# Second stage of a two-layer attention and S4D kernel: convolutions and the kernels' transform on sixteen 32x32 tiles of TensorE

## The chip, the core and the metric

One of the eight NeuronCores of a Trainium2 chip runs the whole program. Its engines work side by side, each through its own queue in order: TensorE multiplies matrices (PE; its weight loads are PEld), ScalarE (ACT) and VectorE (DVE) work on rows of 128 partitions, GpSimd (POOL) does the same from SBUF alone, and SyncE (SP) issues most of the DMAs. The metric is the device time of one execution in microseconds; what counts is the median of several runs.

## The reference, cut to what matters

A sequence of 2048 positions and 640 channels goes through attention (32 heads of 20), an S4D layer, attention, an S4D layer. Each layer adds its result to x.

```python
def _B_ref(u, log_A_real, A_imag, C_real, C_imag, log_dt, D_skip):
    L = u.shape[1]
    dt = jnp.exp(log_dt)
    A = -jnp.exp(log_A_real) + 1j * A_imag
    C = (C_real + 1j * C_imag) * dt[:, None]
    P = jnp.exp((A * dt[:, None])[:, :, None] * pos[None, None, :])
    K = 2.0 * jnp.einsum("dn,dnl->dl", C, P).real
    L2 = 2 * L
    Kf = jnp.fft.rfft(K, L2)
    Uf = jnp.fft.rfft(u_t, L2)
    y = jnp.fft.irfft(Uf * Kf[None, :, :], L2)[:, :, :L]
    return y + u * D_skip[None, None, :]

x = x + _A_ref(_layernorm(x, axis=-1), A_wqkv, A_wo)
x = x + _B_ref(_layernorm(x, axis=-1), ...)
x = x + _A_ref(_layernorm(x, axis=-1), A_wqkv, A_wo)
x = x + _B_ref(_layernorm(x, axis=-1), ...)
```

The convolution kernel K (640 x 2048) depends on the parameters alone and is the same in both S4D layers. The inputs here make none of its parts vanish, so it is computed in full.

## The kernel before

The program runs in six stretches: the first attention, with `kgen` (K by powers of A, written to the DRAM tensor `kd`) woven into it; the first output projection `out_proj`, with `ktransform` (the Fourier transform of K) woven into it; the first convolution `ssm`; the second attention; its output projection; the second convolution.

**The convolution.** The transform of length 4096 is done in two stages over 16 sub-sequences. Channels come in five blocks of 128 (`b`, NCT = 5), and a block has 32 groups of four channels, taken four groups at a time: eight steps per block (`q`), forty in all (`n`). In `ssm`, a step holds

- `stage1`: twelve matmuls against `e1` (float16, high and low parts) give a pair of sub-sequences of the next block; ACT casts the high part into `x1`, DVE subtracts for the low part;
- `stage2a`: eight transposes of `x1` into PSUM (`pst`, pool T), copied by ACT into `xt`;
- `stage2b`: three matmuls of the 128x128 matrix `f2` with 512 columns of `xt` (`psx`, pool F). `f2` holds a 32x32 matrix four times over, once for each of four channels, and zeros elsewhere. Then the product with the kernel's transform, whose two halves `ka` and `kb` are loaded from `kha` and `khb` (256 KB each): DVE shuffles and multiplies, POOL multiplies and adds, giving `t1`;
- `stage3`: the inverse's first part, four float32 matmuls against `fa` (`psv`, pool M), copied by ACT into `v`;
- `stage4`: the inverse's second part, every other step, sixteen matmul passes on four sub-sequences against `eb` (`psy`, pool M). DVE adds the result to x and, in the first convolution, takes the statistics of the next layer norm; in the second, SP writes the output.

`stage2b` runs one step behind the transposes, `stage3` three, `stage4` eleven.

**The kernels' transform.** `ktransform` does the same first two stages for K, once, in float32 where `ssm` has float16 pairs: transposes by time (`pkt` from `kl`, L1245), the first stage (`pkx`, L1257), transposes (`pkt` from `kx`, L1265), the second stage (`pkf`, L1273), two shuffles and a sign on ACT into `kn`, and 512 KB writes to `kha` and `khb`.

**What sets the order.** Instructions are emitted in the order of the code, and a scheduler then places them on each engine by when it expects them ready, unless they are tied: `tie(made, before)` fixes that one instruction comes after another on its engine. In the attentions everything is tied by a plan. `out_proj`, `ktransform` and `ssm` were not tied: `weave(1000)` emits the whole transform after row 2 of the projection, and the scheduler mixes it with the projection's rows. A generator that is woven gives up control at each `yield`; `weave(1)` advances it by one step.

In the profile a tile name without its number stands for all its buffers, and L78 is the helper `Ordered`, through which most operations of ACT, DVE, POOL and SP go.

## Time and profile before

| what | us |
|---|---|
| three runs | 2668.82, 2673.26, 2675.07 |
| their median | 2673.26 |
| the profiled execution | 2672.17 |
| its span, first to last instruction | 2670.4 |
| first attention (0 to 1091) | 1091.0 |
| first projection, transform of K, layer norm (1091 to 1275.4) | 184.4 |
| first convolution (1275.4 to 1416) | 140.6 |
| second attention and projection (1416 to 2509.7) | 1093.7 |
| last layer norm, second convolution, output (2509.7 to 2670.4) | 160.7 |

Of the span, PE is busy for 2528.2 us (95%), ACT for 2368.0 (89%), DVE for 1511.7 (57%), POOL for 824.4 (31%). The stretches are cut at the first transposes of a convolution (`pst`, L1395), at its last `psy`, and at the ends of the attentions' matmuls. A group's row gives its engine, operation, what it writes and reads, the shape, and after the bar its busy time in us and the mean duration of one in ns. A duration holds the passage through the engine too, and the next instruction may start before it is over; what a piece costs an engine is read from start to start.

### The profile page before, as it was taken

To read this page: it belongs to the slowest core of one execution; us is meant where nothing else is said; L and a number is where in the kernel's file an instruction comes from. 1 tells how busy PE (TensorE), PEld (TensorE's weight loads), DVE (VectorE), ACT (ScalarE), POOL (GpSimd) and SP (SyncE) were. 2 spreads that over 40 slices of the span, in tenths; PEclk is the share of its full clock that TensorE was granted. 3 is DMA by queue.
4 is the path that set the end of the run, shared out by engine and by line. 5 is a ranking of instruction groups with operands and counts; after the bars stand their busy time and mean duration, and the time that the engine had idled before them with its cause. 6 is when DMAs were issued, how large, how long until landed. Compare 5 with 4: busy or idle time off the path is not lost.

```text
span 2670.4 us, 116325 instructions
## 1 busy us (share of the span) xinstructions
PE 2528.2 (95%) x51106; PEld 1424.3 (53%) x51106; DVE 1511.7 (57%) x3451; ACT 2368.0 (89%) x2793; POOL 824.4 (31%) x1256
## 2 busy tenths in 40 slices
PE   7899999999999998999999999999999998999898
PEld 3445444444444443678896444454444443444788
DVE  7687778778855884477776323232233221154864
ACT  7899999999999999676655899999999999998564
POOL 1123334233332334301671122322222222222376
PEclk9999999999999999999999999999999999999999
DMA  6523222222221223554542111121121112222465
GB/s 210 182 52 86 59 78 71 75 61 70 63 54 49 55 64 93 191 231 158 186 151 63 47 53 50 53 58 47 43 63 38 54 32 92 70 67 64 143 189 161
DMA packets 186580, 242.18 MB, mean 91 GB/s; under 512 B 43376, under 2 KB 128976, under 8 KB 184400
## 3 DMA queue, kind: packets, MB, share of 16 engines
q1 hardware_dynamic: 150048, 188.35, 21.7%
q0 software_dynamic: 36016, 46.30, 7.0%
q8 instruction: 403, 6.60, 1.0%
q14 instruction: 113, 0.93, 0.1%
HBM read 158.50 MB, written 76.01 MB: 88 GB/s over the span
## 4 chain that ended last, share of the span: by engine, by line
ACT 58%; PE 21%; issue 11%; DVE 3%; DMA 2%; POOL 1%; SPq 0%; ACTq 0%; POOLq 0%; DVEq 0%
ACT pt L78 56%; PE psv L1420 3%; PE psy L1430 3%; PE pa L893 2%; PE psx L1408 2%; PE S L859 2%; PE psx L1385 1%; PE po L1313 1%; PE pst L1395 1%; PE pkf L1273 1%; PE m L611 1%; PE po L1308 1%; PE pq L764 1%; PE pkx L1257 1%; PE pkt L1265 1%
## 5 line engine op out<-in xcount | busy, mean ns | idle before, releaser
L78 ACT ACTIVATE pt<-S 128x1024 f32<-128x1024 f32 x2048 | 1927.8, 1034 | 34.3 <-PE S L859 22.3
L893 PE MATMUL pa<-pt,V 64*32 64x512 f32 x16384 | 1097.5, 590 | 0.2 <-DVE oc L78 0.2
L859 PE MATMUL S<-qop,kop 61*32 61x512 f16 x16384 | 877.7, 381 | 84.7 <-ACT pt L78 67.6
L859 PEld LDWEIGHTS <-kop 61*32 61x32 f16 x16384 | 366.9, 90 | 737.5 <-issue 617.9
L893 PEld LDWEIGHTS pa<-pt,V 64*32 64x32 f32 x16384 | 313.7, 106 | 70.9 <-issue 10.0
L78 POOL DMA_DIRECT2D dn<-oc x252 | 123.8, 498 | 604.6 <-DVE oc L78 580.1
L78 DVE TENSOR_SCALAR qc<-m 128x512 f32<-128x512 f32 (+1 forms) x68 | 46.8, 688 | 285.2 <-PE m L611 282.7
L78 POOL DMA_DIRECT2D db<-dn x252 | 127.0, 510 | 131.6 <-DMA dn<-dr 128.6
L78 DVE COPY oc<-pa 128x512 f32<-128x512 f32 x64 | 44.2, 690 | 197.9 <-PE pa L893 186.9
L78 POOL DMA_DIRECT2D ot<-oc x256 | 130.1, 516 | 81.3 <-DVE oc L78 49.9
L611 PE MATMUL m<-xh,wh 64*32 64x512 f16 x2560 | 144.7, 379 | 2.4 <-DVE qc L78 2.4
L611 PE MATMUL m<-xh,wl 64*32 64x512 f16 x2560 | 145.8, 378 | 0.0
L611 PE MATMUL m<-xl,wh 64*32 64x512 f16 x2560 | 144.3, 378 | 0.0
L611 PEld LDWEIGHTS <-wh 64*32 64x32 f16 x5120 | 90.7, 94 | 76.3 <-issue 34.6
L78 POOL DMA_DIRECT2D dn<-dr x63 | 35.0, 555 | 302.6 <-DVE dr L78 283.9
L78 ACT COPY xt<-pst 128x1024 f16<-128x1024 f16 x80 | 81.6, 1023 | 47.2 <-PE pst L1395 46.7
L1413 POOL TENSOR_TENSOR t<-t,kb 128x512 f32<-128x512 f32 x80 | 101.9, 1275 | 67.7 <-DVE t L78 66.7
L78 DVE TENSOR_SCALAR V<-m 128x160 f32<-128x160 f32 x64 | 20.7, 324 | 161.6 <-PE m L577 161.6
L78 DVE TENSOR_TENSOR kb<-ktab 128x512 f32<-128x512 f32 x160 | 106.2, 682 | 0.0
L577 PEld LDWEIGHTS <-xh 128*128 128x128 f16 x960 | 79.5, 98 | 45.9 <-issue 29.9
L1414 POOL TENSOR_TENSOR t<-t,t 128x512 f32<-128x512 f32 x78 | 99.2, 1271 | 8.5 <-DVE t L78 2.6
L329 PEld LDWEIGHTS m<-kb,ka 128*32 128x32 f32 x3840 | 61.3, 110 | 73.8 <-issue 55.8
(305 smaller groups left out, 4015.3 us busy)
## 6 DMA issues: line engine op xcount, KB each, us to landing
ka<-kha SPq DMA_DIRECT2D x80, 256.0 KB
kb<-khb SPq DMA_DIRECT2D x80, 256.0 KB
db<-dn POOLq DMA_DIRECT2D x252, 64.0 KB, 3.0
kop<-ks SPq DMA_DIRECT2D x176, 80.0 KB
kpw<-wd POOLq DMA_DIRECT2D x60, 192.0 KB, 4.5
qop<-qs SPq DMA_DIRECT2D x256, 40.0 KB
ot<-oc POOLq DMA_DIRECT2D x256, 40.0 KB, 2.8
kha<-kn SPq DMA_DIRECT2D x20, 512.0 KB
```

The costliest lines, as they stand in the source:

```text
L78: made = f(out, *a, **k)
L329: chain(te.matmul(ps[32 * j:32 * j + 32, c8, :], a[n][:, ch, :], b[n][:, dd, :], start=(n == 0), stop=(n == 2), tile_position=(0, 32 * j)))
L577: chain(te.matmul(ps[:, :n], a_[:, ct, sl], m[:, ct, :], start=(k == 0), stop=(k == 14)))
L611: chain(te.matmul(ps[r][32 * t:32 * t + 32, :], a_[rows, ct, 32 * u:32 * u + 32], m[rows, ct, 512 * v:512 * v + 512], start=(k == 0), stop ...
L764: te.matmul(pq, a_[:, ct, :], m[:, ct, sl], start=(n == 0), stop=(n == 14))
L859: chain(te.matmul(S[32 * t:32 * t + 32, 512 * r:512 * r + 512], kt_[rows, kc + 32 * t:kc + 32 * t + 32], qt[rows, :], start=True, stop=Tru ...
L893: chain(te.matmul(pa[r][32 * j:32 * j + 32, :], V[rows, kt, VP * h:VP * h + 32], pts[j // 2][rows, 512 * (j % 2):512 * (j % 2) + 512], sta ...
L1408: te.matmul(px, f2[:, f, :], xt[:, k, :], start=(n == 0), stop=(n == 2))
L1413: ge.tensor_mul(t2, t2, kb)
L1414: (ge if g0 else ve).tensor_add(t1, t1, t2)
L1420: te.matmul(pv[:, g].rearrange("p r i c -> p (r i c)"), t1[:, g * P:g * P + P], fa, start=True, stop=True)
L1430: te.matmul(py[:, i, :], eb[:, 4 * i4 + i, r, :], v[:, r, 4 * i4 + i].rearrange("p g c -> p (g c)"), start=(r == 0), stop=(r == 1))
```

## The change

It touches `ktransform`, `out_proj`, `ssm`, `prefetch`, the constants and, a little, `kgen`.

1. **Sixteen tiles.** The transposes take their groups with a stride (`of_group`), so that the four channels of a group fall into four blocks of 32 partitions. The second stage (`sets` in `ssm`, `ends` in `ktransform`) then multiplies 32x32 matrices at sixteen positions of the array, four row blocks times four column blocks, with 512 columns each. One set in `ssm` is 48 small matmuls in three passes and stands in place of four steps' twelve matmuls; its result fills four PSUM banks (`F0` to `F3`), for which pool T is gone: `pst` now shares pool X with the first stage.
2. **No shuffles in the transform.** `kha` and `khb` are produced by matmuls with two constant matrices; ACT and DVE only copy.
3. **Equal steps.** In `ssm` every engine's order is fixed by `at`. `stage4` works on two sub-sequences in each step instead of four in every other. The inverse's first part runs six steps behind the transposes (two behind the product), the second part fourteen. `xt` and `t2` have one buffer, `ka` five, and the product is written over `ka`.
4. **The transform step by step.** In `out_proj` each eighth projection matmul advances `ktransform` by one of its seventy steps, and the matmuls and transposes of both are tied into one chain on PE; what is left follows the last row. `kl`, `f2` and the skip weights of the first block are loaded before the first attention ends.
5. In `kgen` the scale of K (`bound`) is computed two blocks later.

```diff
-    kha = dram.tile([P, D // 4, P], F32, name="kha")
+    kha = dram.tile([2 * NCT, P, 4, 4, P], F32, name="kha")
...
+    def matmul(*a, **k):
+        chain(te.matmul(*a, **k))
...
-        slow.append((1, bound))
         load_powers(2)
+        slow.append((3, bound))
...
+            def small():
+                sy.dma_start(kl0[1], dsk)
+                sy.dma_start(kl0[2], c_f2.rearrange("p (s m) -> p s m", s=2))
+            rest.extend((small, lambda: load_kl(0)))
...
+    def of_group(x1, g):
+        return x1[:, :, :, :, g].rearrange("p c i s -> p (c i s)")
...
+            def ends(t, xt, s, dst):
+                px = [pst("F", [P, 512], F32, tag=f"F{ch}", name=f"pkf{ch}") for ch in range(4)]
+                for ch in range(4):
+                    rows = slice(32 * ch, 32 * ch + 32)
+                    for g in range(4):
+                        matmul(px[ch][32 * g:32 * g + 32, :].rearrange("p (q k) -> p q k", k=P), f2[rows, s, :],
+                               xt[rows, :, g, :], start=True, stop=True, tile_position=(32 * ch, 32 * g))
+                for h in range(2):
+                    kn = c2.tile([P, 2, 4, P], F32, name=f"kn{s}")
+                    for ch in range(2):
+                        (se.copy if ch else ve.tensor_copy)(kn[:, ch], px[2 * h + ch].rearrange("p (q k) -> p q k", k=P))
+                    sy.dma_start(dst[2 * b + t][:, 2 * h:2 * h + 2], kn)
+            steps = [(turned, 0, xts[0], 0), (turned, 0, xts[0], 1), (by_time, b + 1, 0), (ends, 0, xts[0], 0, kha),
+                     (turned, 1, xts[1], 0), (ends, 0, xts[0], 1, khb), (turned, 1, xts[1], 1), (by_time, b + 1, 1),
+                     (ends, 1, xts[1], 0, kha), (first_stage, b + 1, 0), (ends, 1, xts[1], 1, khb),
+                     (first_stage, b + 1, 1), (first_stage, b + 1, 2), (first_stage, b + 1, 3)]
...
+        def mm(*a, **k):
+
+            if filler[0] is None:
+                te.matmul(*a, **k)
+                return
+            matmul(*a, **k)
+            many[0] += 1
+            if many[0] % 8 == 0:
+                weave(1)
...
-                if s == 2:
-                    weave(1000)
...
         while due:
             ln(*due.pop(0))
-
+        weave(1000)
...
+            def sets(xt):
+                px = [pst("F", [P, 512], F32, tag=f"F{ch}", name=f"psx{ch}") for ch in range(4)]
+                for n, (f, k) in enumerate(((0, 0), (0, 1), (1, 0))):
+                    for ch in range(4):
+                        rows = slice(32 * ch, 32 * ch + 32)
+                        for g in range(4):
+                            mm(px[ch][32 * g:32 * g + 32, :].rearrange("p (q k) -> p q k", k=P), f2[rows, f, :],
+                               xt[rows, k, :, g, :], start=(n == 0), stop=(n == 2), tile_position=(32 * ch, 32 * g))
+                return px
...
+            def product(px, ka, kb, alone):
+                t2 = c1.tile([P, 512], F32, name="t2")
+                at("dve", ve.stream_shuffle(t2, px, SWAP))
+                at("dve", ve.tensor_mul(ka, px, ka))
+                for f, *a in (("tensor_mul", kb, t2, kb), ("tensor_add", ka, ka, kb)):
+                    if alone:
+                        at("dve", getattr(ve, f)(*a))
+                    else:
+                        at("pool", getattr(ge, f)(*a))
+                return ka
...
+            for n in range(NQ + 15):
                 b, q = divmod(n, 8)
+                if n % 4 == 0 and 4 <= n <= NQ:
+                    px = sets(xt)
                 if n < NQ:
...
+                    if n % 4 == 0:
+                        xt = c1.tile([P, 2, 4, 4, P], F16, name="xt")
+                    stage2a(x1, q, xt)
+                if 2 <= n < NQ + 2:
+                    ks[n - 2] = factors(*divmod(n - 2, 4))
+                if sums:
+                    sums[0]()
+                if 4 <= n < NQ + 4:
+                    t1s[n - 4] = product(px[n % 4], *ks.pop(n - 4), n > NQ and n % 2 == 1)
                 if n < NQ and b + 1 < NCT:
                     if q == 0:
                         nxt = new_x1()
-                    stage1(b + 1, nxt, q)
...
+                    stage1(b + 1, nxt, q)()
+                if sums:
+                    sums[1]()
+                    sums = None
+                if 6 <= n < NQ + 6:
...
+                    stage3(vs[m // 2], m % 2, ch, t1s.pop(n - 6))
+                if 14 <= n < NQ + 14:
+                    bb, i2 = divmod(n - 14, 8)
+                    sums = stage4(bb, vs[bb], i2)
...
-                    psum(c3, M=2, T=2, F=2)
+                    psum(c3, M=2, F=1)
```

How it moves instructions, at three places. First DVE in the middle of the first convolution, two steps before the change (`x_...<-psx` is the first stage's subtraction, `t` the product, `x<-x,psy` the sum):

```order
L78 STREAM_SHUFFLE t_29483<-psx 128x512
L78 TENSOR_TENSOR t_29482<-psx,ka 128x512
L78 TENSOR_TENSOR x_29176<-psx_29488,x_29175 128x4x32x4
L78 STREAM_SHUFFLE t_29530<-psx 128x512
L78 TENSOR_TENSOR t_29529<-psx,ka 128x512
L78 TENSOR_TENSOR x_29176<-psx_29535,x_29175 128x4x32x4
L78 TENSOR_TENSOR x<-x,psy 128x4x128
L78 BN_STATS st_28671<-x 128x6 x4
```

and two steps with it:

```order
L78 TENSOR_TENSOR x<-x,psy 128x2x128
L78 STREAM_SHUFFLE t_29903<-psx_29785 128x512
L78 TENSOR_TENSOR ka<-psx_29785,ka 128x512
L78 TENSOR_TENSOR x_29858<-psx_29908,x_29857 128x4x4x32
L78 BN_STATS st_28884<-x 128x6 x2
L78 TENSOR_TENSOR x<-x,psy 128x2x128
L78 STREAM_SHUFFLE t_29952<-psx_29786 128x512
L78 TENSOR_TENSOR ka<-psx_29786,ka 128x512
```

Every step now has one sum of half the width at its head, and its statistics at its end; the four results of one set (here psx_29785 and psx_29786) are used up one per step.

Second, PE in the projection, second block of the transform, before:

```order
L1265 MATMUL pkt<-ident,kx_26927 128x128 x8
L1313 MATMUL po<-wol,oh 128x320
L1313 MATMUL po<-woh,oh 128x320
L1313 MATMUL po<-wol,oh 128x320
L1273 MATMUL pkf<-kxt,f_26628 128x512
L1265 MATMUL pkt<-ident,kx_26927 128x128 x4
L1273 MATMUL pkf<-kxt,f_26628 128x512
```

and with the change, between two stretches of eight projection matmuls:

```order
L196 MATMUL pkt<-ident,kx_25866 128x128 x8
L193 MATMUL po<-woh,oh 128x320
L193 MATMUL po<-wol,oh 128x320
L193 MATMUL po<-woh,ol 128x320 x6
L193 MATMUL pkf_26873<-kxt_25869,f_25865 32x512 x4
L193 MATMUL pkf_26874<-kxt_25869,f_25865 32x512 x4
L193 MATMUL pkf_26875<-kxt_25869,f_25865 32x512 x4
L193 MATMUL pkf_26876<-kxt_25869,f_25865 32x512 x4
```

Where four transposes and one 128x128 matmul took turns, a step of eight transposes or of sixteen small matmuls stands alone, with eight projection matmuls on either side.

Third, PE behind the projection's last row, where nothing of the transform stood before and where the first convolution's first stage followed at once:

```order
L196 MATMUL pkt<-ident,kx_25866 128x128 x16
L193 MATMUL pkf_28733<-kxt_25869,f_25865 32x512 x4
L193 MATMUL pkf_28734<-kxt_25869,f_25865 32x512 x4
L193 MATMUL pkf_28735<-kxt_25869,f_25865 32x512 x4
L193 MATMUL pkf_28736<-kxt_25869,f_25865 32x512 x4
L196 MATMUL pkt<-ident,kx_25866 128x128 x8
L193 MATMUL pkf_28773<-kxt_25869,f_25865 32x512 x4
```

These, two more sets, and three steps of the first stage ahead of them (`pkx`) are what the sixty advances leave over for the last block.

More of the change, by code (lines that the diff above doesn't have):

```diff
@@ new lines, in first_stage, with block, turned @@
+                            matmul(ps[:, r, i, :], e1[:, e, s, r, :], m[:, s, :], start=(n == 0), stop=(n == 2))
+                (ve.tensor_copy if i2 % 2 else se.copy)(by_channel(x1, i2), ps.rearrange("p r i (c g) -> p (r i) c g", c=4))
+        def block(b):
+            def turned(t, xt, h):
+                for q in (2 * h, 2 * h + 1):
+                    pt = pst("X", [P, 4, P], F32, tag="X", name="pkt")
+                    for g in range(4):
+                        transpose(pt[:, g, :], of_group(x1, 16 * t + 4 * q + g), ident)
+                    if q % 2:
+                        ve.tensor_scalar_mul(xt[:, q], pt, ksc[:, 1:2])
+                    else:
+                        se.activation(xt[:, q], pt, AF.Copy, scale=ksc[:, 1:2])
+            def ends(t, xt, s, dst):
[14 more added lines that the diff above has]
+                     (first_stage, b + 1, 1), (first_stage, b + 1, 2), (first_stage, b + 1, 3)]
+            for f, *a in steps:
+                if f in (turned, ends) or b + 1 < NCT:
+                    f(*a)
+                    yield
@@ L1283, in ktransform @@
+        for h in range(2):
+            by_time(0, h)
+            yield
+        for n in range(4):
+            first_stage(0, n)
+            yield
         for b in range(NCT):
-            yield from unit_load(b)
+            yield from block(b)
         c.close()
@@ L1373, in ssm, with at, mm @@
             c3 = c.enter_context(tc.tile_pool(name="s3", bufs=3))
+            order = {}
+            def at(name, made):
+                order[name] = tie(made, order.get(name))
+            def mm(*a, **k):
+                at("pe", te.matmul(*a, **k))
             eb = c1.tile([P, NI, 2, P], F32, name="eb")
```

217 lines of the change are left out of this document (85 added, 132 removed).

## The prediction

> **What bounds the kernel now.** I read the chain of waits first (the page's part 4), then windows cut at the edges of the stages that the diff touches, then the instructions of those stages in order of time.
>
> ```profile
> ACT 58%; PE 21%; issue 11%; DVE 3%; DMA 2%; POOL 1%; SPq 0%; ACTq 0%; POOLq 0%; DVEq 0%
> core 0: us, PE busy (x) PEld busy (x) DVE busy (x) ACT busy (x) POOL busy (x), PEclk, DMA share, GB/s
> 1093.30:1264.20 170.90, 167.42 (x1288) 138.79 (x1283) 128.27 (x346) 112.99 (x181) 29.61 (x32) 1.00 0.50 185
> 1264.20:1275.40 11.20, 8.27 (x128) 7.25 (x127) 10.40 (x25) 8.22 (x15) 2.04 (x2) 1.00 0.51 156
> 1275.40:1415.60 140.20, 137.80 (x1434) 122.99 (x1434) 101.86 (x259) 81.69 (x151) 104.69 (x93) 1.00 0.48 154
> 1305.00:1362.70 57.70, 57.70 (x627) 51.84 (x626) 42.46 (x105) 35.21 (x64) 41.19 (x34) 1.00 0.48 150
> 2524.20:2663.70 139.50, 137.00 (x1407) 121.51 (x1407) 84.92 (x170) 80.44 (x148) 99.97 (x79) 1.00 0.60 189
> ```
>
> ScalarE's 58% of the chain is the softmax of the two attentions, which the change leaves alone. TensorE's 21% lies in three places that it does touch: the first output projection with the kernels' transform woven in (1093.3 to 1264.2) and the two convolutions (1275.4 to 1415.6, 2524.2 to 2663.7). In the middle of a convolution (1305 to 1362.7, sixteen steps) PE is busy for all 57.70 us, while DVE, ACT and POOL have slack. So there a microsecond of PE saved is a microsecond won, until another engine takes over. Between 1264.2 and 1275.4 the last layer norm is waited for.
>
> Two steps of that middle, in order of time (start, duration):
>
> ```profile
> 1306.69 0.61 PE L1395 MATMUL pst<-id,x 128*128 128x128 f16 x8
> 1307.14 0.81 PE L1408 MATMUL psx<-xt,f2s 128*128 128x512 f16 x3
> 1307.79 0.22 PE L1385 MATMUL psx<-uh,e1s 128*128 128x128 f16 x1
> 1308.46 1.11 PE L1420 MATMUL psv<-fa,t 128*128 128x128 f32 x8
> 1309.40 0.61 PE L1395 MATMUL pst<-id,x 128*128 128x128 f16 x8
> 1309.85 0.81 PE L1408 MATMUL psx<-xt,f2s 128*128 128x512 f16 x3
> 1310.50 0.22 PE L1385 MATMUL psx<-uh,e1s 128*128 128x128 f16 x1
> 1311.17 1.11 PE L1420 MATMUL psv<-fa,t 128*128 128x128 f32 x8
> 1312.11 1.95 PE L1430 MATMUL psy<-v,eb 128*128 128x128 f32 x16
> 1313.90 0.61 PE L1395 MATMUL pst<-id,x 128*128 128x128 f16 x8
> ```
>
> The difference of starts is what a piece costs PE: transposes 0.45, second stage 0.65 (three matmuls of 512 columns, 0.217 each), first stage 0.67, inverse's first part 0.94, inverse's second part 1.79 every other step. Two steps are 7.21 us, one 3.61.
>
> **The sixteen tiles.** The second stage's 128x128 matrix is mostly zeros; now 32x32 pieces stand in it, sixteen at a time, and a set of 48 small matmuls does in three passes what four steps did in twelve. No 32x32 matmul of this length is in the trace. The nearest rows are attention's 64x32 tiles, eight at a time.
>
> ```profile
> L859 PE MATMUL S<-qop,kop 61*32 61x512 f16 x16384 | 877.7, 381 | 84.7 <-ACT pt L78 67.6
> 1600.73 1.06 PE L893 MATMUL pa<-pt,V 64*32 64x512 f32 x16
> 1601.59 0.41 PE L859 MATMUL S<-qop,kop 61*32 61x512 f16 x8
> 1601.94 0.24 PE L577 MATMUL m<-vh,xh 128*128 128x160 f16 x1
> 1602.43 0.23 PE L577 MATMUL m<-vl,xh 128*128 128x160 f16 x1
> 1602.60 0.41 PE L859 MATMUL S<-qop,kop 61*32 61x512 f16 x8
> ```
>
> Eight scores of 381 ns each together last 0.41 us, so their starts spread over 0.03 us and they run side by side. The eight float32 ones take 0.86 us (1600.73 to 1601.59), no more than one pkf of the same length below. Going over to 128x128 costs 0.35 - 0.217 = 0.13 (1601.59 to 1601.94); going back, 0.10 (the last L577 starts at 1602.43 and streams 160 columns, 0.07). Sixteen should start within 0.06, so a set costs 3 x 0.217 + 0.06 + 0.23 = 0.94 us per four steps, 0.24 per step instead of 0.65. The bound above is that sixteen run as two eights, 0.65 more per set. Below, 0.65 with no switch seen. I take 0.94, since nothing in the rows for eight hints at a limit.
>
> By the Trainium skill, "TensorE: Matmul & The Clock Gate", section "Wait — 56ns, not 53.3ns?", starts of matmuls never come closer than about 25 ns; the eight starts within 0.03 us disagree. By that rule an estimated pass of sixteen would take 0.40 us, and the sum would be 11 us longer. No run here shows sixteen yet.
>
> The transposes now read every 32nd element of x1 as weights. The trace has such reads in float32 only, next to a contiguous one:
>
> ```profile
> 1145.08 0.44 PE pkt L1265 x4
> 1145.52 0.45 PE pkt L1245 x4
> 1185.77 0.92 PE pkf L1273 x2
> 1186.69 0.44 PE pkt L1265 x4
> 1187.13 0.86 PE pkf L1273 x2
> 1221.42 1.35 PE pkx L1257 x24
> 1247.73 2.93 PE po L1313 x20
> 1250.66 1.58 PE po L1308 x10
> ```
>
> L1245 reads every 16th element and takes 0.45 where L1265, contiguous, takes 0.44. So I take 0; were the loads twice as long, 0.45 x 80 steps = 36 us would be lost.
>
> **The convolution, step by step.** In full steps PE now needs 3.61 - 0.65 + 0.24 = 3.20 us. Do the others keep up?
>
> ```profile
> L1413 POOL TENSOR_TENSOR t<-t,kb 128x512 f32<-128x512 f32 x17 | 21.7, 1276 | 15.3 <-DVE t L78 15.3
> L1414 POOL TENSOR_TENSOR t<-t,t 128x512 f32<-128x512 f32 x17 | 21.6, 1273 | 1.3
> L78 ACT COPY xt<-pst 128x1024 f16<-128x1024 f16 x16 | 16.3, 1021 | 13.3 <-PE pst L1395 13.1
> L78 DVE STREAM_SHUFFLE t<-psx 128x512 f32<-128x512 f32 x16 | 11.8, 737 | 0.1
> L78 DVE TENSOR_TENSOR x<-psx,x 128x512 f16<-128x512 f32 x17 | 11.6, 679 | 0.0
> L78 DVE TENSOR_TENSOR t<-psx,ka 128x512 f32<-128x512 f32 x16 | 10.8, 673 | 0.0
> L78 ACT COPY v<-psv 128x256 f32<-128x256 f32 x32 | 10.3, 375 | 5.8 <-PE psv L1420 5.8
> L78 ACT CAST x<-psx 128x512 f16<-128x512 f32 x16 | 9.4, 585 | 3.4 <-PE psx L1385 3.4
> L78 DVE BATCH_NORM_STATS2 st<-x 128x6 f32<-128x128 f32 x32 | 7.0, 280 | 0.3
> ```
>
> POOL: 1.276 + 1.273 = 2.55. ACT: 1.02 + 0.59 + 2 x 0.38 = 2.36. DVE: 0.74 + 0.67 + 0.68 + 2 x 0.28 = 2.65, and the add of the half-size result, not in the trace, between nothing and the 0.69 that the whole one would take by the row for the subtraction of the same width; halfway with a start-up, 0.42. That is 3.07 of 3.20, tight in the first convolution; the second has no statistics. The product lags its set by up to four steps, the inverse lags the product by two (6.4 us against POOL's 2.55 plus DVE's 1.4), and the loads of ka and kb are asked for two steps ahead with POOL's release in between; at the 0.48 DMA share of the middle they stay hidden. Without that cover each step would wait up to POOL's 2.55.
>
> The edges are worse than before. The transposes and the first stage now share two X buffers (T is gone), so one first-stage result must be cast and subtracted before the next starts: 0.67 + 0.59 + 0.68 and three hand-overs of about 0.12 make a ring of 2.3 us. So, from the first transposes to the last psy:
>
> - steps 0 to 5 (no inverse yet): 6 x 2.3 + 0.94 = 14.7
> - steps 6 to 13 (inverse's first part joins; POOL's 2.55 sets the pace): 8 x 2.6 = 20.8
> - steps 14 to 31: 18 x 3.20 = 57.6
> - steps 32 to 39 (no first stage; PE 2.53, POOL 2.55): 8 x 2.6 = 20.8
> - steps 40 to 45 (inverse only, some products on DVE alone): 0.94 + 6 x (0.94 + 0.90) = 12.0
> - steps 46 to 53: 8 x 0.90 + 1 for the last copies = 8.2
>
> 134.1 us against 140.2 and 139.5: 6.1 + 5.4 = 11.5 won. PE alone would give 40 x 0.41 = 16.4 each; the ring and POOL take the rest.
>
> **The kernels' transform.** Per block of five, PE before: sixteen by-time transposes 1.8, 96 first-stage matmuls in eight units 5.4 (1.35 for two units), 32 transposes 3.5, eight pkf of 0.87 = 7.0. Sixteen rows of the projection are 16 x 4.51 = 72.2. In all 72.2 + 5 x 17.7 = 160.7 of the window's 170.9, so 10.2 is stall. Now pkf is four sets of 0.86 + 0.06 + 0.23 = 1.15, so 4.6 per block: 5 x 2.4 = 12.0 saved. The two shuffles and the sign's activation become plain copies, fewer in sum on ACT and DVE, and the writes to kha and khb stay forty of the same size.
>
> PE's order is now fixed: one step of the transform behind each eight projection matmuls (1.18 us), and 480 of these give sixty steps of seventy, so about eleven are left behind the last row. PE on those: 3 x 1.35 + 4 x 0.88 + 4.6 = 12.2. Before the last row stand 160.7 - 12.0 - 12.2 = 136.5 of work, and stalls. I take 13, a little above the 10.2, since PE cannot step round a late copy; bounds are 0 and half a microsecond on each of the sixty steps, 30. The last row is then done at 1093.3 + 149.5 = 1242.8. Behind it 12.2, some six waits for a copy (0.74 by the shuffle's row plus 0.2) and seven first-stage units of 0.67: 22.5, with the last layer norm's 11.2 under it. Transposes start at 1265.3 instead of 1275.4: 10 won.
>
> The rest costs nothing: the scale's seven small DVE operations and the earlier load of kl lie under the first attention's softmax (ACT's 58%); uncovered, the 1 MB load would cost under 6 us at 185 GB/s.
>
> Sum: 11.5 + 10 = 21.5, against the profiled execution's 2672.2: 2650.7. The runs' median of 2673.3 is 1.1 above it; I forecast **2651.5 us**.
>
> **Rivals.**
>
> *PE is the only limit.* For it: 57.70 busy of 57.70. Against it: the X ring and POOL's 2.55. The convolutions would win 16.4 each, and the transform 12.0 + 11.2 + some stalls, 25: 2673 - 58 = 2615.
>
> *Sixteen tiles run as two eights, or start too slowly.* Twenty sets lose 0.65, 13 in all; the float32 sets are long enough to hide it: 2664. Against it: the 0.03 us for eight starts.
>
> *The fixed order stalls the projection.* Each projection matmul now queues on PE behind a transform step that waits for copies, and these stand on ACT and DVE behind the layer norm's. For it: DVE is busy for 128.27 of 170.9 and a copy behind two others takes 0.2 + 3 x 0.74 = 2.4, against 1.18 of projection between steps. If half of the sixty steps lose 1.2, that is 36 on top of the 13: 2687, slower than before. It decides from about 27 us, 0.45 per step. Against it: the copies before had more work and PE lost only 10.2.
>
> **How the numbers follow.** Forecast 0.66 (its own range 2636 to 2668), PE-only 0.12, two eights 0.08, stalls 0.12, and 0.02 for the strided weights' 36 us, which end at the same time. About 0.2% (2667.9 and 2678.6) is what can be told from no change. Faster: 0.63 of the forecast's, 0.12 and 0.05, so 0.80; same: 0.03 + 0.02 + 0.03 = 0.08; slower: 0.01 + 0.11 = 0.12. The range is 2622 to 2680: it leaves out the best end of PE-only and the worst stalls, 2 in 10 at most.
>
> **What would show it.** Right: sets that start 0.9 us apart from the transposes behind them, full steps of 3.2 us, the first convolution near 134 us, transposes from about 1265. Wrong: pst matmuls more than 0.06 us apart (strided weights), a set over 1.3 us (no sixteen side by side), projection matmuls idle behind kxt, kx or kn copies (fixed order), or full steps over 3.3 with PE waiting for DVE.

## The result, and the profile after

The changed kernel takes 2674.7 us (median of 12 runs, 2672.0 to 2683.1) against 2672.3 for the kernel before (12 runs beside it): ratio 1.0014, 95% interval 1.0004 to 1.0024. Some 21 us were forecast as won, and nothing is.

The profiled execution has a span of 2671.8 us (2670.4 before). First the chain of waits of the changed kernel, by engine:

```profile
ACT 57%; PE 19%; issue 13%; DMA 5%; DVE 4%; POOL 1%; SPq 0%; ACTq 0%; POOLq 0%; DVEq 0%
```

PE fell from 21% to 19%, but DMA rose from 2% to 5% and issue from 11% to 13%: matmuls went, waits came. Where, shows the view by windows of the changed kernel, cut at the first matmul of the projection, its last one, the convolution's first transposes and its end, then eighteen middle steps of it, and the second convolution:

```profile
core 0: us, PE busy (x) PEld busy (x) DVE busy (x) ACT busy (x) POOL busy (x), PEclk, DMA share, GB/s
1093.87:1259.64 165.77, 148.72 (x1611) 126.53 (x1612) 110.42 (x243) 84.24 (x138) 31.87 (x37) 0.94 0.47 168
1259.64:1283.70 24.06, 19.91 (x329) 14.57 (x327) 17.21 (x34) 14.74 (x26) 0.00 (x0) 1.00 0.56 220
1283.70:1420.70 137.00, 128.77 (x1824) 121.41 (x1824) 106.56 (x288) 81.84 (x154) 101.72 (x90) 1.00 0.53 171
1319.20:1377.40 58.20, 58.20 (x842) 56.12 (x840) 47.60 (x124) 39.20 (x74) 47.22 (x38) 1.00 0.53 169
2527.70:2665.00 137.30, 129.83 (x1824) 122.34 (x1824) 92.28 (x196) 81.42 (x152) 96.52 (x76) 0.99 0.67 204
```

| stretch, us | before | predicted | after |
|---|---|---|---|
| projection's first matmul to its last | 170.9 | 149.5 | 165.8 |
| from there to the first transposes | 11.2 | 22.5 | 24.1 |
| first convolution | 140.2 | 134.1 | 137.0 |
| second convolution | 139.5 | 134.1 | 137.3 |

The convolutions gave 3.2 and 2.2. The first transposes start at 1283.7 instead of 1275.4, which takes 8.3. Another 1.6 came back between the convolutions (which part of the second attention gave it was not tried): 8.3 - 3.2 - 1.6 - 2.2 = 1.3, the span's 1.4. The first attention's last matmuls end at 1093.4 in the kernel before, not at 1091 as its table of stretches has it, and at 1091.8 in the changed kernel. In the kernels below that end lies between 1090.8 and 1095.4, but for one, so a stretch is compared from its own start.

**The sixteen tiles do what they should.** The order in time on TensorE in the middle of the changed kernel's first convolution (start, duration):

```profile
1325.44 0.92 PE L1412 MATMUL psx<-xt,f2s 32*32 32x512 f16 x48
1326.30 0.71 PE L1433 MATMUL pst<-id,x 128*128 128x128 f16 x8
...
1327.51 1.11 PE L1412 MATMUL psv<-fa,ka 128*128 128x128 f32 x8
1328.46 1.06 PE L1412 MATMUL psy<-v,eb 128*128 128x128 f32 x8
1329.35 0.65 PE L1433 MATMUL pst<-id,x 128*128 128x128 f16 x8
...
1338.42 0.92 PE L1412 MATMUL psx<-xt,f2s 32*32 32x512 f16 x48
```

A set of 48 takes 0.86 us from its start to the next transposes; from set to set it is 12.98, four steps of 3.25. The middle has no idle time on PE.

**The projection's beginning does not.** VectorE of the changed kernel around the end of the first attention, in its order:

```profile
1064.07 0.69 DVE L78 TENSOR_TENSOR oc<-oc,db 128x512 f32<-128x512 f32 x1
1091.82 0.16 DVE L78 TENSOR_TENSOR kl<-kl,skip 128x1 f32<-128x1 f32 x1 [27.07 <-DMA kl<-kd]
1091.90 0.17 DVE L78 TENSOR_SCALAR dr<-dr 128x16 f32<-128x16 f32 x1
...
1104.95 0.69 DVE L78 TENSOR_TENSOR oc<-oc,db 128x512 f32<-128x512 f32 x1 [9.89 <-DMA dn<-oc]
1105.56 0.75 DVE L78 SCALAR_TENSOR_TENSOR ktrl<-pkt,ksc,ktrh 128x512 f16<-128x512 f32 x1
1106.22 0.82 DVE L78 TENSOR_TENSOR ol<-otl,oh 128x640 fp32r<-128x640 f32 x1
```

The same two operations in the kernel before:

```profile
1081.96 0.17 DVE L78 TENSOR_SCALAR dr<-dr 128x16 f32<-128x16 f32 x1 [8.84 <-DMA dr<-dn]
1094.80 0.69 DVE L78 TENSOR_TENSOR oc<-oc,db 128x512 f32<-128x512 f32 x1
```

Before the change, `dr` (the softmax's reciprocals) ran at 1082.0 and the multiplication of `oc` by `db`, their broadcast, at 1094.8. Now they run at 1091.9 and 1104.95, and the transform's `ktrl` and the second row's `ol` stand behind. TensorE pays, as its order shows, and pays again by its clock (PEclk, the last column but two of the windows; times in the four windows of half clock):

```profile
1093.87 1.70 PE L193 MATMUL po<-woh,ol 128*128 128x320 f32 x8 [2.08 <-DVE ol L78]
1106.36 1.12 PE L196 MATMUL pkt<-ident,kl 128*128 128x128 f32 x4 [7.44 <-DVE ktrl L78]
```

```profile
1094.80:1098.20 3.40, 3.40 (x17) 3.36 (x16) 0.25 (x1) 1.38 (x2) 3.40 (x8) 0.50 0.94 297
1101.60:1111.80 10.20, 5.07 (x25) 4.50 (x26) 5.05 (x8) 1.38 (x2) 2.59 (x5) 0.50 0.54 143
1224.50:1227.90 3.40, 3.40 (x22) 3.20 (x20) 1.67 (x3) 0.00 (x0) 1.22 (x1) 0.50 0.00 0
1248.40:1251.80 3.40, 3.31 (x16) 2.90 (x14) 1.96 (x4) 1.38 (x2) 0.23 (x1) 0.50 0.58 230
```

If half of the busy time in them is lost, that is (3.40 + 5.07 + 3.40 + 3.31) / 2 = 7.6 us, an estimate: in these windows `po` matmuls start 0.27 us apart, and 0.15 at full clock. Before, the mean clock of this stretch was 1.00.

**Later in the projection** TensorE idles in six more places, 8.4 us in sum. The two largest waits (sum, times, longest; the sixth place is 0.7 for `kn`), and ScalarE ahead of one such place:

```profile
PE pkx L193 <- ACT kx L78: 4.3, 3, 2.1
PE pkt L196 <- ACT kxt L78: 3.4, 2, 2.6
```

```profile
1243.44 1.74 ACT L78 ACTIVATE u<-x,nb,rs 128x640 f32<-128x640 f32 x2 [2.64 <-DVE nb L78]
1245.09 1.34 ACT L78 CAST uh<-u 128x640 f16<-128x640 f32 x2
1246.33 1.06 ACT L78 COPY kn<-pkf 128x512 f32<-128x512 f32 x2
1247.29 0.69 ACT L78 ACTIVATE kxt<-pkt,ksc 128x512 f32<-128x512 f32 x1
```

The copies that TensorE needs were ready to run, but stood on ScalarE behind the layer norm's `u`, which waited for VectorE.

VectorE in turn waited for `kl` again. The chain of waits ahead of another of the six places:

```profile
1138.43 5.81 DMA kl<-kd
1144.26 0.16 DVE kl L78
1144.99 1.74 ACT u L78 x2
1147.87 0.58 ACT kx L78
```

The change loads `kl` into one buffer where the kernel before had two. Three later loads hold VectorE's queue for 3.8 us in sum (2.4 before, in two), with the layer norm's operations behind. No run took this out.

### The profile page after: what moved, and what is told of

Same layout as the page of the kernel before. It is cut to its first block, busy times and chain, and to the rows that moved or that the text cites. A ratio compares the mean times of both kernels' runs of the same rounds, so it can differ in the third digit from the quotient of the medians.

```text
span 2671.8 us, 118793 instructions
## 1 busy us (share of the span) xinstructions
PE 2496.7 (93%) x52386; PEld 1412.8 (53%) x52386; DVE 1510.4 (57%) x3407; ACT 2344.9 (88%) x2763; POOL 817.3 (31%) x1250
## 4 chain that ended last, share of the span: by engine, by line
ACT 57%; PE 19%; issue 13%; DMA 5%; DVE 4%; POOL 1%; SPq 0%; ACTq 0%; POOLq 0%; DVEq 0%
ACT pt L78 54%; PE psy L1412 3%; PE psv L1412 2%; PE pa L900 2%; PE psx L1412 2%; PE po L193 2%; PE S L866 2%; PE pst L1433 1%; DMA kl<-kd 1%; DVE x L78 1%; PE pkt L196 1%; PE pq L771 1%; PE m L618 1%; DMA qop<-qs 1%; PE pkx L193 1%
## 5 line engine op out<-in xcount | busy, mean ns | idle before, releaser
L1461 POOL TENSOR_TENSOR kb<-t,kb 128x512 f32<-128x512 f32 x76 | 97.1, 1278 | 84.8 <-DVE t L78 46.0
L1461 POOL TENSOR_TENSOR ka<-ka,kb 128x512 f32<-128x512 f32 x76 | 97.4, 1281 | 6.0
```

Of the source, the lines that this page charges most:

```text
L1461: at("pool", getattr(ge, f)(*a))
```

## The experiments

Each kernel is the changed one with the edit shown. Ratios are to the kernel before, run beside it (2672.1 to 2673.4 us).

**Free order** (`e1_free`). The ties of `matmul` and `transpose` go, and the whole transform is emitted at row 2:

```diff
-            matmul(*a, **k)
-            many[0] += 1
-            if many[0] % 8 == 0:
-                weave(1)
+            te.matmul(*a, **k)
...
+                if s == 2:
+                    weave(1000)
```

> The ties of TensorE's order in the first output projection and the kernels' transform are gone, and the whole transform is emitted at the projection's third row, as in the kernel before; tiles, copies and convolutions stay those of the changed kernel. Theory 'fixed order': the changed kernel loses 16 us of idle TensorE and 8 us of halved clock in this stretch only because TensorE cannot step round a late copy. Then most of it comes back, the first convolution's transposes start near 1270 instead of 1283.7, and the time is near 2660. Rival 'copies': ScalarE and VectorE set the pace of the stretch in any order, the transposes start within 3 us of 1283.7, and the time stays within 3 us of 2674.7.

2692.6 us, ratio 1.0076 (1.0064 to 1.0088). Both readings fall; this order is 18 us worse than the changed kernel's. The scheduler put the transform first and more than eight rows' worth of projection last, the stretch took 206 us, and the early idle time is there as well, with no transform step at that place (the ties and the place of the transform changed together, so neither has a price of its own):

```profile
1106.43 1.97 PE L1327 MATMUL po<-woh,ol 128*128 128x320 f32 x6 [8.58 <-DVE x L78]
```

**Steps later and denser** (`e2_late6`), **denser from the start** (`e3_seven`):

```diff
-            if many[0] % 8 == 0:
+            if many[0] > 60 and many[0] % 6 == 0:
```

> One step of the transform behind each six projection matmuls, and the first only behind the second row, so that all seventy steps stand before the last row. Theory 'early steps': the first two steps stand in VectorE's order behind copies that wait for a DMA; with them go the 9.9 us idle around 1092 to 1108 and 4 us of halved clock, the transposes start near 1270, and the time is near 2661. Rival 'the stall moves': the denser steps wait more behind ScalarE's layer norm copies, and the time stays over 2670.

> One step of the transform behind each seven projection matmuls instead of eight, from the start as in the changed kernel, so that the tail behind the last row has about two steps instead of eleven. Theory 'tail': the 24 us between the last row and the first transposes shrink to the 11 of the kernel before and the time falls by about 10, to 2665. Rival 'work only moved': the eleven steps cost TensorE as much ahead of the last row as behind it, where the last layer norm lies over them; the last row ends 12 us later, the tail is 12 us shorter, and the time stays within 3 us of 2674.7.

2676.8 us, 1.0017 (1.0008 to 1.0026), and 2676.2, 1.0014 (1.0005 to 1.0023). With the first step behind the second row, TensorE still idled 2.3 and 6.9 us, now ahead of `po`: the first steps are not the cause, the projection itself waits, and the time is that of the rival. With every seventh, the last row ended at 1273.3 instead of 1259.6 and the tail took 14.7 instead of 24.1: the work is moved, not hidden, as the rival had it.

**Free convolutions** (`e4_loose`): `at` returns its instruction untied.

> The ties of the convolutions' instructions on TensorE, ScalarE, VectorE, POOL and SyncE are gone; the program's order of emission stays, and the scheduler may move instructions past each other. Theory 'ties cost the edges': the second convolution's head (2.9 us idle behind the last row's cast, 4 us at half clock) shrinks, and the time falls by 3 to 6 us. Rival 'ties hold the steps equal': the steps of the middle grow past 3.25 us, and the time rises by 3 us or more.

2748.2 us, 1.0279 (1.0266 to 1.0292). The first convolution took 152.1 us instead of 137.0. The rival holds, far beyond its 3 us: the equal steps live by the ties.

**kl asked for earlier** (`f1_kl_first`), **the generator's steps undone** (`f2_kgen_back`):

```diff
-            rest.extend((small, lambda: load_kl(0)))
+            rest[1:1] = [small, lambda: load_kl(0)]
```

> The first load of kl is asked for right behind the first quarter of x instead of behind all of x; nothing else moves. Theory 'late kl': in the changed kernel VectorE waits 27 us for that load at its addition of the skip weight, and behind it stand the softmax's reciprocals, whose broadcast then lands 10 us late and holds up the projection's second row; with the load early the 7.4 us idle near 1099 to 1106, most of the 2.1 us ahead of the first row and some 4 us of halved clock go, the first convolution's transposes start 8 to 13 us earlier, and the time is near 2664. Rival 'another wait is behind it': the projection's first rows wait for their own loads or for the broadcast anyway, and the time stays within 3 us of 2674.7.

> The kernels' generator gets its steps back as they were before the change: the three maxima in one step instead of three, and the scale worked out with the second block instead of the fourth. Theory: these steps make the loads of the output weights, x and kl start 12 us later (1048.7 instead of 1036.9), and that is why kl lands only at 1091.7; undone, kl lands near 1080, VectorE's wait falls under the attention's last blocks, and the time is near 2664. Rival: the generator ends as late as in the changed kernel for another reason, the loads start within 3 us of 1048.7, and the time stays within 3 us of 2674.7.

The first took 2688.7 us, 1.0057 (1.0044 to 1.0071), and neither reading holds. Asked for only 2.5 us earlier, the load let the scheduler place the skip addition still further ahead on VectorE, in front of the copy that empties the attention's result:

```profile
1081.13 0.16 DVE L78 TENSOR_TENSOR kl<-kl,skip 128x1 f32<-128x1 f32 x1 [37.05 <-DMA kl<-kd]
1081.36 0.69 DVE L78 COPY oc<-pa 128x512 f32<-128x512 f32 x1
```

TensorE idled 17.4 us for that copy, the attention ended 20.5 us later (1112.3 instead of 1091.8), and from the first row to the first transposes it was 187.2 instead of 189.8. The second took 2674.2, 1.0012 (1.0002 to 1.0022): the loads started at 1047.7 instead of 1048.7, so the rival holds and the generator's steps are not the cause.

**u on VectorE** (`f3_u_dve`):

```diff
-                        ln_u(..., uh, ul, up2, not general)
+                        ln_u(..., uh, ul, up2, early)
```

> In the first projection the normalised row u is made on VectorE instead of ScalarE. Theory 'ScalarE's head': in six places TensorE idles 0.7 to 2.6 us, 8.4 in sum and 3.4 at halved clock, because ScalarE waits at u for the layer norm's small operations on VectorE while copies of transform results stand behind it; with u on VectorE ScalarE's copies go on, and the time falls by 6 to 10, to 2666. Rival 'VectorE is as full': its queue takes sixteen more operations of about 0.7 us, the same stalls come back behind VectorE's copies, and the time is 2674 or more.

2668.9 us, 0.9990 (0.9979 to 1.0001), 6 us below the changed kernel. The first reading holds: the two later half-clock windows are gone, and from the first row to the first transposes it took 185.3 instead of 189.8.

**Transposes in the inverse's buffers**, for fourteen steps (`f4_ring14`) and six (`g4_ring6`):

```diff
-                pt = pst("X", [P, 2, 4, P], F16, tag="X", name="pst")
+                pt = pst("M" if early else "X", ..., tag="mm" if early else "X", name="pst")
```

> In a convolution's first fourteen steps the transposes write to the two buffers of the inverse instead of the two that they share with the first stage. Theory 'X ring': these two shared buffers make the 2.27 us of each of the first six steps (13.6 us) and 2.74 of the next eight (21.9); with them apart the six take about 1.7 each and the eight 2.6, so 4 to 5 us less per convolution, and the time is near 2666. Rival 'copies': ScalarE's two copies and VectorE's subtraction of a step set the pace, or the wait moves to the inverse's buffers, and each phase stays within 1 us.

> As the run with the inverse's buffers for the transposes, but in the first six steps alone, in which the inverse has no results yet. Theory 'X ring': those six steps fall from 13.6 to 10 in the first convolution and from 13.9 to 11 in the second, as they did there, and the next eight keep their 21.9 and 21.4 instead of 24.6 and 22.1; 6 us less, near 2668. Rival 'the pipeline fills later anyway': the six steps are shorter but the next eight wait for VectorE, ScalarE and POOL by as much as was won, and the sum of the fourteen stays within 1.5 us per convolution.

2674.8 us, 1.0007 (0.9998 to 1.0016), and 2673.7, 1.0005 (0.9996 to 1.0014). With six, the first six steps fell from 13.6 to 10.9 us (second convolution 13.9 to 11.3), so the shared buffers did set them (fourteen steps gave 9.8, and 24.6 for the eight). But the next eight rose from 21.9 to 23.9 (21.3 to 21.9): 0.7 of the first convolution's 2.7 stayed, and 2 of the second's 2.6. The ring reading holds for the six steps, the rival for most of the first convolution's sum. By their times neither kernel can be told from the changed one: the intervals overlap with its 1.0004 to 1.0024.

**The skip addition tied behind the softmax** (`g1_kl_tie`), **three edits together** (`g2_all`: this, `u`, six steps):

```diff
+                    scales.append(ve.tensor_mul(oc, oc, db[0]).ins)
...
+                if b == 0:
+                    tie(made, scales[-2])
```

> The first addition of the skip weight is tied behind the last but one multiplication of oc by db on VectorE, so that the softmax's reciprocals no longer stand behind the load of kl; the load itself stays where it is. Theory 'late kl': the reciprocals run near 1081 instead of 1091.9, the broadcast db lands about 10 us earlier, the first row starts within 0.5 us of the attention's last matmul (idle 2.1 before), the 7.4 us idle ahead of the first transposes' second half falls under 2, and with them 4 to 6 us of halved clock; the first convolution's transposes start 10 us earlier counted from the attention's end, and the time is near 2663. Rival 'the stretch is bound elsewhere': the idle time goes at this place and comes back at later ones, as in the run with the early load, whose stretch from first row to first transposes took 187.2 us against 189.8; then the time falls by less than 4.

> Three edits together: the first skip addition tied behind the softmax's operations, u of the first projection on VectorE, and the first six steps' transposes in the inverse's buffers. If each acts at its own place, their gains add: 10 or 11 us from the tie, 4 to 6 from u, 6 from the buffers, together about 20 less than the changed kernel, 2654, faster than the kernel before by 18. If the projection's stretch has another bound (its rows and ScalarE's and VectorE's copies), the first two give no more than 6 together, and the time is near 2663.

2677.6 us, 1.0015 (1.0005 to 1.0026), and 2667.1, 0.9977 (0.9968 to 0.9986). `g2_all` lies near its second reading: the gains do not add up to its 2654. In the first run the late `kl` was only the last of several late things. With it out of the way `dr` waited for its own load until 1087.7, `db` came as late as ever, and TensorE idled 9.7 us at the same place. The theory fell; the cause lies further up.

**The place of the buffers** (`h1_mem_tie`, with the tie; `h2_mem_all`, with all edits). In the changed kernel the loads of the output weights (`wot`) wait on SP, and the softmax's `dn<-oc` stands on POOL behind the splitting of these weights:

```profile
SPq L78 <- DMA kd<-ko: 13.0, 1, 13.0
```

```profile
1072.77 1.54 POOL L1187 TENSOR_TENSOR wol<-wot,woh 128x640 fp32r<-128x640 f32 x1
1074.26 2.16 POOL L78 DMA_DIRECT2D dn<-oc  x4
```

The same places in the kernel before:

```profile
1036.89 2.47 SPq L78 DMA_DIRECT2D wot<-in_wo  x5
1065.65 1.92 POOL L78 DMA_DIRECT2D dn<-oc  x4 [1.14 <-DVE oc L78]
```

No wait for `kd<-ko` was there before. `kd<-ko` is the last store of the kernels' generator. The change takes `kl`, `kx1`, `ktr` and `kxt` (48 KB of each partition) from the pool `w1` ahead of the weights' staging tiles, so these slide, as the wait says, into memory that the generator still uses, and their loads start at 1048.7 instead of 1036.9. The edit takes the same tiles from a pool that is opened only after that of the staging tiles is closed:

```diff
-            kl0[:] = [w1.tile([P, L], F32, name="kl"), ...]
             with tc.tile_pool(name="wos", bufs=NCT, side="right") as ws:
...
+            w3 = c.enter_context(tc.tile_pool(name="wo3", bufs=1, side="right"))
+            kl0[:] = [w3.tile([P, L], F32, name="kl"), ...]
```

> The transform's buffers (kl, skip, f2, kx1, ktr, kxt) lie behind the staging tiles of the output weights instead of ahead of them, and the first skip addition is tied as in the run before. Theory 'place of the buffers': ahead of the staging tiles they push these into the memory of the kernels' generator, so that the load of wot waits for the generator's last store (1048.7 instead of 1036.9), POOL splits the weights 12 us later, the softmax's dn<-oc stands behind that on POOL, and db lands at 1103 instead of 1094. With the buffers behind, wot loads near 1037, db lands by 1096, the idle 7 to 9.7 us of the projection's second row goes with 4 us of halved clock, and the time is near 2664. Rival 'POOL's order': wot loads early, but POOL's or the queues' order keeps dn<-oc as late as it is, db lands after 1102, and the time stays within 4 us of 2675.

> The place of the buffers and the tie as in the other run of this call, with u of the first projection on VectorE and the first six steps' transposes in the inverse's buffers. If the early stall goes by the buffers' place, this is 8 to 12 us faster than the run of all three edits before it, near 2657, and 0.6% faster than the kernel before; if it does not, it stays within 3 us of 2667.

2669.2 us, 0.9988 (0.9979 to 0.9996), and 2663.5, 0.9961 (0.9949 to 0.9972). SP, VectorE and the windows of `h1_mem_tie`:

```profile
1038.88 2.47 SPq L78 DMA_DIRECT2D wot<-in_wo  x5
```

```profile
1096.81 0.69 DVE L78 TENSOR_TENSOR oc<-oc,db 128x512 f32<-128x512 f32 x1
```

```profile
1095.32:1256.32 161.00, 145.77 (x1617) 123.54 (x1612) 110.32 (x244) 84.10 (x138) 29.86 (x33) 0.98 0.48 169
1256.32:1280.39 24.07, 19.93 (x328) 14.58 (x327) 17.22 (x34) 14.72 (x26) 0.00 (x0) 1.00 0.56 220
```

`db` no longer keeps VectorE waiting, the long early stall is gone, and from the attention's last matmul to the first transposes are 185.0 us instead of 191.9 (192.2 with the tie alone, in `g1_kl_tie`). The two kernels with the tie differ by the buffers' place alone, and their intervals lie apart. The theory holds, at 5.5 us of total instead of 11: waits of 0.9, 0.8, 0.7 and 3.0 stand at that place now. SP still waits 16.4 us for `kd<-ko`, but ahead of the load of `otl`, which starts at 1064.9 (1062.6 before the change). The buffers' place without the tie was not run. `h2_mem_all` is 3.5 us faster than `g2_all` where its first reading had 8 to 12, and their intervals overlap: a copy `kx` on VectorE, behind the softmax's reciprocals, holds TensorE for 3.4 us there, with 6.8 us at half clock.

**The next queue heads** (`k1_kx_act`, `k2_uh_pool`), on top of `h2_mem_all`: the first block's `kx` copies on ScalarE; then `uh` of rows 0 to 13 cast on POOL.

```diff
-                (ve.tensor_copy if i2 % 2 else se.copy)(by_channel(x1, i2), ...)
+                (ve.tensor_copy if i2 % 2 and b else se.copy)(by_channel(x1, i2), ...)
...
-            se.copy(uh[:, s, :], u)
+            (se.copy if on_act or s >= NI - 2 else ge.tensor_copy)(uh[:, s, :], u)
```

> As the fastest run so far (buffers behind the staging tiles, tie, u on VectorE, first transposes in the inverse's buffers), and the eight copies kx of the first block all on ScalarE. Theory: of that run's early idle time 3.4 us and 6.8 us at half clock follow from a kx copy that stands on VectorE behind the softmax's reciprocals, which wait for a DMA until 1105.7; with the copy on ScalarE they go, 5 us, to 2658.5. Rival: the additions of the projection's results to x stand behind the same reciprocals, TensorE waits for its po buffers instead, and the time stays within 2 us of 2663.5.

> As the other run of this call, and uh of the first projection's rows 0 to 13 is cast on POOL instead of ScalarE. Theory: the remaining idle places of 0.5 to 2 us, 7.7 in sum, are waits for kx and kxt copies on ScalarE behind casts that wait for u; with the casts on POOL they go, and this is 5 us faster than the other run. Rival: POOL's cast delays its subtraction, and so the last rows, or the copies are late behind VectorE's u instead; the two runs are within 2 us of each other.

2660.5 us, 0.9957 (0.9944 to 0.9971): 3 us less, between the two readings, and the interval overlaps with that of `h2_mem_all`. The 3.4 us wait became one of 2.2 for VectorE's addition to x, as the rival had it, but the half clock at that place went. Then 2656.0, 0.9940 (0.9926 to 0.9953): 4.5 us less, near the theory's 5, though the two intervals overlap a little. The half clock is back for 3.4 us there, behind an idle time of 2.18 us, where `k1_kx_act` had none behind 2.17. **This is the fastest version, 16 us under the kernel before** and by the ratios still further under the changed one. What TensorE waits for between its rows now, and the windows of the stretch:

```profile
PE po L193 <- DVE x L78: 6.0, 6, 2.2
PE pkx L193 <- DVE kx L78: 0.7, 1, 0.7
```

```profile
1092.65:1245.25 152.60, 143.16 (x1617) 121.98 (x1612) 114.83 (x247) 66.19 (x113) 43.73 (x47) 0.99 0.50 179
1245.25:1269.96 24.71, 19.92 (x328) 14.63 (x327) 17.71 (x34) 13.91 (x25) 0.00 (x0) 1.00 0.55 214
```

ScalarE is out of the list, and the rows take 152.6 us, near the 149.5 of the prediction.

**Keeping TensorE busy** (`w1_warm`), on top of `h2_mem_all`:

```diff
+            if last:
+                order["pe"] = rowend[0]
+                warm_up(52)
             for i2 in range(8):
+                if last and i2 == 5:
+                    warm_up(60)
```

> As the fastest run so far, and at the head of the second convolution TensorE does 112 transposes of the identity whose results nothing reads: 52 behind the projection's last matmul and 60 ahead of the sixth first-stage unit. This work is added and computes nothing. Theory 'idle halves the clock': in every run the granted clock falls to 0.5 for 3.4 or 6.8 us behind TensorE's idle time there; with the transposes in that idle time it stays 1.00 from 2512 to 2535, and the first three steps are 1.5 to 2 us shorter. Rival: the clock falls at fixed times or by the load of other engines, and the rows of half clock stay. The total changes by less than can be told, 2661 to 2664.

2669.7 us, 0.9990 (0.9981 to 0.9999), 6 us worse than without, which neither reading had. The first 52 took over the projection's buffers, waited 3.3 us for them, ran at half clock and pushed the first stage back. The other 60 did fill the second wait. The same 61 matmuls, from the first transposes to the fourth, in `w1_warm` and then in `h2_mem_all`:

```profile
2527.06:2531.23 4.17, 3.92 (x61) 3.66 (x61) 1.31 (x3) 2.94 (x5) 0.00 (x0) 1.00 0.46 170
```

```profile
2521.96:2527.41 5.45, 5.37 (x61) 5.12 (x62) 1.73 (x3) 3.51 (x5) 0.00 (x0) 0.64 0.83 344
```

The clock stays at 1.00 where the idle time is filled, and the three steps are 1.3 us shorter. A high DMA load alone does not halve it: from 2516.1 to 2530.0 of `w1_warm` the clock is 1.00 at DMA shares of 0.80 and 0.82. The theory holds for the second idle time; for the first, which was not filled, it is untested. Here the work cost more than it gave.

## Why the prediction was wrong, step by step

- **Sixteen tiles.** Right: 0.86 measured for 0.94. The rival of two eights is refuted. The rule of the Trainium skill, "TensorE: Matmul & The Clock Gate", section "Wait — 56ns, not 53.3ns?", that starts never come closer than about 25 ns, does not hold here for matmuls on different tiles: 48 starts at 25 ns would be an estimated 1.2 us.
- **Strided transposes.** Nearly right: first transposes to first stage takes 0.48 to 0.54 instead of 0.45, some 3 to 4 us over all, not 36. With this a full step is 3.25 for 3.20.
- **The convolutions.** Right in mechanism, 3 us short each. In the order of the prediction's phases the first took 13.6, 21.9, 58.2, 20.8, 14.1 and 8.4 for 14.7, 20.8, 57.6, 20.8, 12.0 and 8.2. That the first two misses cancel is luck; the largest is the end, steps 40 to 45, where I had summed TensorE's work and left out its waits for ScalarE's copies of `v`. No run took these waits out; they are read from the changed kernel (sum, times, longest):

```profile
PE psy L1412 <- ACT v L78: 2.2, 3, 0.7
```

  Won are 5.4 where I had 11.5. That the X buffers set the first six steps was shown by `g4_ring6`.
- **pkf.** Right: 1.07 for 1.15.
- **"Before the last row stand 160.7 - 12.0 - 12.2 = 136.5 of work, and stalls. I take 13".** Here the sum came out short. Measured: 165.8 to the last row, of which 16.2 are waits for copies, some 7.6 are lost to the halved clock, and 142.0 are the rest. So waits and clock are 23.8 where 13 stood, and the half clock was in no term at all. The rest is 5.5 above the 136.5: eight projection matmuls between two steps mostly take 1.28 us to the next piece (1216.93 to 1218.21 is one) where the sum counts 1.20, some 5 us over sixty steps, and the sum had no term for the switch.
- **The reason given for the 13, "since PE cannot step round a late copy".** Not borne out: without the ties, and with the transform emitted in one go, the kernel is slower still (1.0076), and the early stall is there without a step of the transform. As shown by `f3_u_dve`, `h1_mem_tie`, `k1_kx_act` and `k2_uh_pool` together, the stalls come from what stands at the head of VectorE's, ScalarE's, POOL's and SP's queues.
- **"The rest costs nothing: the scale's seven small DVE operations and the earlier load of kl lie under the first attention's softmax (ACT's 58%)".** This is the step that failed. The operations cost nothing (`f2_kgen_back`), but I priced the load of `kl` by its bytes and not by where its buffer lies. `h1_mem_tie` shows it: with the tile taken after the staging tiles, and the tie, the stretch is 6.9 us shorter than in the changed kernel, and 7.2 shorter than with the tie alone. Further, the `u`, `uh` and `kx` queue heads: from `h1_mem_tie` to `k2_uh_pool` the rows fall from 161.0 to 152.6.
- **The tail.** 24.1 for 22.5, right; `e3_seven` shows that the eleven steps cost as much ahead of the last row.
- **The rivals.** The measured time lies between "two eights" (2664), which the sets refute, and "the fixed order stalls the projection" (2687), which has the right place. The sign that the prediction named for the latter, matmuls idle behind `kxt`, `kx` or `kn` copies, did come: these are the 8.4 us later in the projection. The early stall is not its mechanism. "PE is the only limit" is refuted by both convolutions, where TensorE is busy for 128.8 of 137.0 and 129.8 of 137.3.
- **Slips of the working that change nothing.** 2673.3 less 21.5 is 2651.8, not 2651.5. And not all of TensorE's 21% of the chain lies in the three places: on the page, `pa` and `S` (2% each) and `m` and `pq` (1% each) belong to the attentions.

With the queue heads cleared, the stretch from first row to first transposes takes 177.3 us (`k2_uh_pool`), 4.8 less than before; the prediction had 10.1 less.

## What to carry to other kernels

A tile that is taken earlier from a stack of pools moves every tile behind it: ask whose memory they now wait for, and follow that wait through the queues of SP, POOL and VectorE to the engine that sets the end. When a wait is cleared and the time stays, look at what its instruction would have waited for next: here the late `kl` hid a late `dn<-oc` on POOL, and that the late weights. And count an idle stretch of TensorE with the slower clock that may follow it.

## What the runs showed of the hardware

- **Sixteen 32x32 tiles run side by side**: 48 float16 matmuls of 512 columns in 0.86 us, change of shape included, where twelve 128x128 ones took 2.6 (12 x 0.217).
- **TensorE's clock can halve for 3.4 us, or a multiple of it, after an idle time as short as 2 us.** Idle times of 2.08, 2.12 and 2.56 us in the changed kernel were followed by 3.4 us at half clock, one of 1.41 was not. One of 2.11 in `h1_mem_tie` and one of 2.17 in `k1_kx_act` were not, while one of 2.18 at the same place in `k2_uh_pool` was: the length alone does not decide. The Trainium skill, "TensorE: Matmul & The Clock Gate", section "HAM oscillation — how this bites in real kernels", warns of gaps over about 3.4 us; here shorter ones were enough. A wait of 2 us can so cost an estimated 1.7 more, half of 3.4.
